# Banded attention in steps of two units instead of one, without the filling product, ahead of two fused MLPs

## The chip, the cores and the metric

One core of one Trainium2 chip runs the whole program. The metric is the device time of one execution in microseconds (us). The engines are TensorE (PE; its weight loads are PEld), VectorE (DVE), ScalarE (ACT), GpSimd (POOL) and SyncE (SP, which here only issues transfers). Each engine works through its own list of instructions in order and waits on semaphores for the others.

## What is computed

Attention over 2 batches and 8 heads of 768 tokens by 64, in which a token sees the 96 latest tokens and the first 8, with a slope per head; then two MLPs over all 1536 tokens. Cut to what matters:

```
scores = q @ k.T / sqrt(D) + bias        # bias: -slope[h] * distance
scores = where(is_global | is_local, scores, -1e9)
a = exp(scores - max);  a = a / (sum(a) + 1e-9)
x = a @ v                                 # (1536 tokens, 512)
h = x @ w_in;  x = (h * tanh(softplus(h))) @ w_out
x = rms_norm(x) * rms_g
out = (silu(x @ w_gate) * (x @ w_val)) @ w_out2
```

## The kernel before

**Units.** Attention goes by units: a unit is one batch b, one pair of heads p (two heads j = 0, 1) and one tile t of 128 queries. A pair has six units, and there are 2 x 4 pairs, so 48 units. Because of the band, a unit with t = 0 has 128 keys and any other 256 (`width`). A unit passes through seven pieces of work: `scores` (TensorE, L639, one product per head into two score banks), `soft` (VectorE L660 adds the bias and takes the row's maximum; ScalarE L670 does the exponential and its sum; each once per head), `norm` (VectorE L685 and L687 make the inverse of the sums, GpSimd L689 multiplies, once per head), `transp` (TensorE L704, four transposes, two for t = 0), `evac` (ScalarE L712 copies the transposed unit out of its bank), `pv` (TensorE L724, the products with the values, into a bank that three units share) and, after the third unit of such a bank, `evac_out`: `split_into` writes the bank as a rounded high part (ScalarE L352) and a low part (VectorE L353, which reads L352's result). Behind each unit's scores TensorE also issues a filling product of 128 x 128 at L647 into the unused end of a score bank; its result is not used.

**The loop.** The loop at L757 runs i from -4 to 49. In loop i the engines get the scores of unit i + 4, the transposes of unit i, the value products of unit i - 2, the evacuation of unit i - 1, the softmax of unit i + 3, the norm of unit i + 2 and the `evac_out` of unit i - 2, written in that order. So the order of each engine's list is fixed by the loop's text. Score banks are two pairs that take turns.

**What is woven in.** Eight pieces of the first weights are converted during attention (`Piece`): mag, clamp, b1, b2, b3, hi, lo, each one pass over 128 x 512 words. `plan` gives each a loop and a slot, and `tick` issues it there. Here mag is on ScalarE (L152), clamp, b1, b2, b3 on VectorE (L160, L163, L169, L175), hi and lo on GpSimd. mag and b3 also issue the transfer of a later weight piece on SP. The transfers of q, k and v of later pairs stand in SP's list too.

**The end.** In its last loops, by `AHEAD`, TensorE also does the first 16 groups of three products of the first MLP (L362). `mish1(0)` is ScalarE's and VectorE's part of the MLP's first half step. What follows, from the first product at L414 on, is the two MLPs.

Of the kernel before, what the change touches and what calls it, by code (L numbers as in the profile page):

```python
# [17 lines left out]
P = 128  # L18
B, H, S, D = 2, 8, 768, 64
NT = S // P  # L20
# [23 lines left out]
AHEAD = {-4: (0, 2), -3: (2, 4), -2: (4, 6), -1: (6, 8), 0: (8, 12), 1: (12, 16)}  # L44
# [6 lines left out]
def tile_attention_mish_swiglu(  # L51
# [74 lines left out]
    class Piece:  # L126
# [16 lines left out]
        def mag(self):  # L143
# [443 lines left out]
    def attention_banded():  # L587
        fresh()
        mm = [mm_bank() for _ in range(4)]
        with ExitStack() as st:  # L590
            qk = st.enter_context(tc.tile_pool(name="a_qk", bufs=2, reuse_waits="tile"))
            bp = st.enter_context(tc.tile_pool(name="a_b", bufs=1, reuse_waits="tile"))
            sm = st.enter_context(tc.tile_pool(name="a_s", bufs=5, reuse_waits="tile"))
            ep = st.enter_context(tc.tile_pool(name="a_e", bufs=5, reuse_waits="tile"))
            pp = st.enter_context(tc.tile_pool(name="a_p", bufs=3, reuse_waits="tile"))
# [31 lines left out]
            sc, ex, pt, po = {}, {}, {}, {}  # L627
# [5 lines left out]
            def scores(u):  # L633
                b, p, t = u
                n = width(t) // P
                banks = mm[2:4] if units.index(u) % 2 else mm[0:2]
                for j in range(2):
                    r = slice(64 * j, 64 * j + 64)
                    pe.matmul(  # L639
                        banks[j][:, 0 : n * P],  # L640
                        qs[b, p][r, t * P : (t + 1) * P],
                        ks[b, p][r, 0, :] if t == 0 else ks[b, p][r, t : t + NT : NT - 1, :],
                        start=True,
                        stop=True,
                    )

                pe.matmul(  # L647
                    banks[1][:, 3 * P :], ones[:, 0:P], ones[:, 0:P], start=True, stop=True
                )
                sc[u] = banks  # L650

            def soft(u, tick):
                b, p, t = u
                n = width(t)
                banks = sc.pop(u)
                e = ep.tile([P, 2, 2 * P], F32, tag="e", name=nm("e"))
                s = sm.tile([P, 4, 2], F32, tag="s", name=nm("s"))
                for j in range(2):
# [18 lines left out]
                    )  # L677
                    tick(j)
                ex[u] = (e, s)

            def norm(u, tick):
                b, p, t = u
                n = width(t)
# [271 lines left out]
```

## Time and profile before

| | |
|---|---|
| Runs shown | 690.1, 689.78, 693.67 us; median 690.1 |
| Profiled execution, its own time | 688.42 us, span 686.6 us |
| TensorE's products, busy | 669.5 us, 98% of the span |
| TensorE's weight loads, busy | 587.1 us, 86% |
| VectorE busy | 450.2 us, 66% |
| ScalarE busy | 385.9 us, 56% |
| GpSimd busy | 68.2 us, 10% |
| TensorE's mean granted clock | 0.997 of full speed |

The shares are means over stages that differ: attention is roughly the first sixth of the span. A busy TensorE is not TensorE at its peak, since products overlap and their ends are modelled; the starts of its weight loads tell its pace better. In the chain of waits each piece is what the next one had to wait for.

### The profile page before, as it was taken

Reading aid. Unit: us, or ns where it says so; the run is one execution under the profiler, and the core shown is the slowest. Engines: PE = TensorE matmul, PEld = TensorE weight load, DVE = VectorE, ACT = ScalarE, POOL = GpSimd, SP = SyncE. Lnnn points to the kernel's source line nnn. Section 1 sums busy time; section 2 is a strip of 40 time slices with the busy share of each in tenths; the row PEclk is TensorE's granted clock in tenths of the full one; section 3 lists DMA queues with packets and bytes.
Section 4 is the critical chain, followed back from the end, with each engine's and each line's share of the span. In section 5 each row is a group of like instructions: output and inputs, shape, how many; then the busy total and the mean of one; then the engine's idle time right before and its main releaser. Section 6 shows DMA issues by size and latency. Waiting matters only on the chain.

```text
span 686.6 us, 10023 instructions
## 1 busy us (share of the span) xinstructions
PE 669.5 (98%) x3760; PEld 587.1 (86%) x3760; DVE 450.2 (66%) x1067; ACT 385.9 (56%) x722; POOL 68.2 (10%) x128
## 2 busy tenths in 40 slices
PE   7999999999999999999989999999999999999997
PEld 3656678999999999999868899999999999999996
DVE  6777865887788778877777778873368774331232
ACT  5888879888888888888888423222122222111111
POOL 3666750000000000000000000000000000000000
PEclk9999999999999999999999999999999999999999
DMA  7967520122113113211212122130022200010111
GB/s 237 304 224 223 160 84 32 67 89 86 67 62 93 62 61 93 63 62 62 84 40 63 42 81 93 62 93 31 1 62 92 93 1 1 0 47 1 46 47 51
DMA packets 26728, 54.20 MB, mean 79 GB/s; under 512 B 2608, under 2 KB 14640, under 8 KB 26672
## 3 DMA queue, kind: packets, MB, share of 16 engines
q1 hardware_dynamic: 25968, 53.16, 24.4%
q8 instruction: 31, 0.51, 0.3%
q10 hardware_dynamic: 704, 0.33, 0.2%
q14 instruction: 25, 0.20, 0.1%
HBM read 50.34 MB, written 3.15 MB: 78 GB/s over the span
## 4 chain that ended last, share of the span: by engine, by line
PE 84%; ACT 7%; DVE 6%; DMA 1%; issue 1%; SPq 0%; DVEq 0%
PE mm L362 45%; PE s L414 31%; PE mm L639 2%; PE s L724 2%; ACT e L670 2%; PE s L704 2%; DVE x L426 1%; ACT s L460 1%; DVE e L660 1%; DMA q<-in_qT_dram 1%; PE mm L273 1%; PE s L443 1%; DVE hl L353 1%; ACT hl L352 1%; PE mm L647 1%
## 5 line engine op out<-in xcount | busy, mean ns | idle before, releaser
L362 PE MATMUL mm<-hl,w 128*128 128x384 f32 x1920 | 349.2, 336 | 0.0
L362 PEld LDWEIGHTS mm<-hl,w 128*128 128x128 f32 x1920 | 336.8, 188 | 7.5 <-issue 1.0
L414 PE MATMUL s<-w,g 128*128 128x512 f32 x1008 | 247.5, 395 | 0.0
L414 PEld LDWEIGHTS s<-w,g 128*128 128x128 f32 x1008 | 188.5, 189 | 36.3
L552 ACT ACTIVATE r<-mm 128x384 f32<-128x384 f32 x48 | 23.5, 490 | 128.5 <-PE mm L362 128.5
L553 DVE TENSOR_TENSOR r<-r,mm 128x384 f32<-128x384 f32 x48 | 26.4, 549 | 65.9 <-ACT r L552 65.9
L426 DVE TENSOR_TENSOR x<-x,s 128x512 f32<-128x512 f32 x60 | 40.4, 687 | 41.0 <-PE s L414 41.0
L488 ACT ACTIVATE g<-r 128x384 fp32r<-128x384 f32 x48 | 25.2, 526 | 68.4 <-DVE r L553 68.4
L391 DVE TENSOR_TENSOR d<-d,mm 128x384 f32<-128x384 f32 x64 | 32.5, 549 | 42.0 <-ACT d L388 42.0
L689 POOL TENSOR_SCALAR e<-e,s 128x256 f32<-128x256 f32 (+1 forms) x96 | 47.6, 508 | 35.3 <-DVE bias L620 10.0
L670 ACT ACTIVATE e<-e,s 128x256 f32<-128x256 f32 (+1 forms) x96 | 46.1, 482 | 7.9 <-DVE s L660 7.6
L169 DVE SCALAR_TENSOR_TENSOR bits<-stage,bits 128x512 int32<-128x512 int32 x68 | 48.2, 709 | 2.1
L175 DVE SCALAR_TENSOR_TENSOR bits<-stage,bits 128x512 int32<-128x512 int32 x68 | 47.2, 694 | 2.0
L488 ACT ACTIVATE g<-d 128x384 fp32r<-128x384 f32 x64 | 33.6, 526 | 21.6 <-DVE d L391 20.0
L492 DVE TENSOR_TENSOR g<-r,g 128x384 fp32r<-128x384 f32 x48 | 26.8, 559 | 28.4 <-ACT g L488 28.4
L386 ACT ACT_TABLE_LOAD x32 | 41.1, 1283 | 0.6
L194 DVE TENSOR_TENSOR w<-bits,w 128x512 fp32r<-128x512 f32 x60 | 41.3, 689 | 0.0
L382 ACT ACTIVATE d<-mm 128x384 f32<-128x384 f32 x64 | 30.5, 491 | 18.7 <-PE mm L362 17.1
L382 ACT ACT_TABLE_LOAD x31 | 39.8, 1283 | 0.5
L190 ACT ACTIVATE w<-bits 128x512 fp32r<-128x512 f32 x60 | 37.0, 616 | 0.0
L639 PE MATMUL mm<-k,q 64*128 64x256 f32 (+1 forms) x168 | 31.9, 411 | 4.7 <-DVE s L660 2.6
L660 DVE CUSTOM_DVE_ANT_0 e<-mm,bias 128x256 f32<-128x256 f32 (+1 forms) x96 | 35.0, 395 | 0.8 <-PE mm L639 0.8
(82 smaller groups left out, 506.2 us busy)
## 6 DMA issues: line engine op xcount, KB each, us to landing
stage<-in_w_out_dram SPq DMA_DIRECT2D x28, 512.0 KB, 3.2
stage<-in_w_in_dram SPq DMA_DIRECT2D x16, 512.0 KB, 3.9
stage<-in_w_gate_dram SPq DMA_DIRECT2D x12, 512.0 KB, 3.4
stage<-in_w_val_dram SPq DMA_DIRECT2D x12, 512.0 KB, 3.5
k<-in_kT_dram SPq DMA_DIRECT2D x7, 704.0 KB, 4.2
out_dram<-x SPq DMA_DIRECT2D x12, 256.0 KB, 2.1
q<-in_qT_dram SPq DMA_DIRECT2D x7, 384.0 KB, 4.9
v<-in_v_dram SPq DMA_DIRECT2D x7, 384.0 KB, 6.1
```

The lines of the kernel that those rows point to most:

```text
L169: dve.scalar_tensor_tensor(self.bits, self.lw, 29, self.bits, op0=ALU.logical_shift_right, op1=ALU.bitwise_or,)
L175: dve.scalar_tensor_tensor(self.bits, self.hw, -1073741824, self.bits, op0=ALU.bitwise_and, op1=ALU.bitwise_or,)
L194: engine.tensor_tensor(self.wt[:, 1, :], self.fl, self.wt[:, 0, :].bitcast(F32), op=ALU.subtract)
L362: pe.matmul(ps[:, 0:BT], w[:, wi, col], xs[kc][:, xi, :], start=kc == 0 and i == 0, stop=kc == NK - 1 and i == 2,)
L382: act.activation(self.t[:, i, :], self.h[i], AF.Tanh, scale=0.5)
L414: pe.matmul(acc[m], gt[:, gi, tok], w[:, wi, :], start=c % 4 == 0 and i == 0, stop=c % 4 == 3 and i == 2,)
L426: dve.tensor_tensor(y, y, acc[m], op=ALU.add)
L488: act.activation(gt[:, 0, :], x, AF.Copy)
L639: pe.matmul(banks[j][:, 0 : n * P], qs[b, p][r, t * P : (t + 1) * P], ks[b, p][r, 0, :] if t == 0 else ks[b, p][r, t : t + NT : NT - 1, :] ...
L660: dve.tensor_tensor_reduce(e[:, j, 0:n], banks[j][:, 0:n], bias0[:, h, :] if t == 0 else bias[:, h, :], scale=-0.125, scalar=3.0e38, op0=A ...
L670: act.activation(e[:, j, 0:n], e[:, j, 0:n], AF.Exp, scale=-1.0, bias=s[:, 0, j : j + 1], accum_out=s[:, 1, j : j + 1],)
L689: pool.tensor_scalar(e[:, j, 0:n], e[:, j, 0:n], s[:, 3, j : j + 1], 0.0, op0=ALU.mult, op1=ALU.add,)
```

## The change

Attention goes by steps of two units (24 steps). A step's scores fill both halves of a head's score bank, k = 0 and 1. Loop i (from -2 to 24) has the scores of step i + 2, the transposes of step i (eight), the value products of step i - 1 (sixteen for full units: two units, two heads, two halves of the keys, each in two passes), then softmax of the first unit of step i + 2, evacuation of the first unit of step i, norm of step i + 1, softmax of the second unit, evacuation of the second, and `evac_out` of step i - 1. There is no filling product. All magnitudes are on VectorE. The slots of the pieces, the buffers, `AHEAD` and the place of `mish1(0)` follow the steps. The old L352, L353, L660, L670, L712, L362 and L414 become L349, L350, L659, L669, L706, L359 and L411.

```diff
-AHEAD = {-4: (0, 2), -3: (2, 4), -2: (4, 6), -1: (6, 8), 0: (8, 12), 1: (12, 16)}
+AHEAD = {-2: (0, 8), -1: (8, 12), 0: (12, 16)}
...
-            if self.i < NW_EARLY:
-                act.activation(self.fl, self.hw.bitcast(F32), AF.Abs)
-            else:
-                dve.tensor_scalar(
-                    self.bits, self.hw, 1, 1,
-                    op0=ALU.logical_shift_left, op1=ALU.logical_shift_right,
-                )
+            dve.tensor_scalar(
+                self.bits, self.hw, 1, 1,
+                op0=ALU.logical_shift_left, op1=ALU.logical_shift_right,
+            )
...
-                pe.matmul(
-                    banks[1][:, 3 * P :], ones[:, 0:P], ones[:, 0:P], start=True, stop=True
-                )
...
+                banks = mm[2:4] if i % 2 else mm[0:2]
+                for k, (b, p, t) in enumerate(steps[i]):
+                    n = width(t)
+                    for j in range(2):
+                        r = slice(64 * j, 64 * j + 64)
+                        pe.matmul(
+                            banks[j][:, 2 * k * P : 2 * k * P + n],
+                            qs[b, p][r, t * P : (t + 1) * P],
...
+                i0 = 1 + k * (ns - 4) // NW_EARLY
+                for op, di, slot in (
                     ("mag", 0, 0),
-                    ("clamp", 1, 2),
-                    ("b1", 2, 0),
-                    ("b2", 2, 2),
-                    ("b3", 3, 1),
-                    ("hi", 3, 3),
-                    ("lo", 4, 3),
+                    ("clamp", 0, 1),
+                    ("b1", 0, 2),
+                    ("b2", 1, 0),
+                    ("b3", 1, 1),
+                    ("hi", 1, 2),
+                    ("lo", 2, 1),
                 ):
...
-            for i in range(-4, nu + 2):
+            for i in range(-2, ns + 1):
...
+                ahead = i + 2 < ns
+                if ahead:
+                    scores(i + 2)
                 if i < 0:
                     warm(bank("s3"), WARM, ones)
...
+                if 0 <= i < ns:
+                    transp(i)
+                if i >= 1:
+                    pv(i - 1)
...
+                if i == ns - 1:
                     mish_first = Mish(first)
...
+                    for c in range(2):
+                        mish_first.tanh(c)
+                if ahead:
+                    soft(i + 2, 0)
+                tick(0)
+                if 0 <= i < ns:
+                    evac(i, 0)
+                if 0 <= i + 1 < ns:
+                    norm(i + 1)
+                tick(1)
+                if ahead:
+                    soft(i + 2, 1)
+                if 0 <= i < ns:
+                    evac(i, 1)
+                if -1 <= i < 5:
+                    make_bias(i + 3)
+                if i >= 1:
+                    evac_out(i - 1)
+                tick(2)
...
-                if i == nu - 1:
+                if i == ns - 1:
                     for piece in pieces:
                         piece.rest()
-                if i == nu:
                     mish1(0, mish_first)
```

ScalarE in the middle of attention, before, around the split of the second value bank of pair (0, 3) (`hl_181`; `e` are the units' exponentials, `pt` their evacuated transposes, "x2" is once per head):

```order
L712 ACTIVATE pt_936<-s_170_902 128x512
L670 ACTIVATE e_938,s_939<-e_938,s_939 128x256 x2
L712 ACTIVATE pt_961<-s_176_929 128x2x128
L670 ACTIVATE e_963,s_964<-e_963,s_964 128x256 x2
L352 ACTIVATE hl_181<-s_171_907 128x384
L712 ACTIVATE pt_988<-s_180_952 128x512
```

The same place in the change, from the split of that pair's first value bank on:

```order
L349 ACTIVATE hl_177<-s_128_765 128x384
L669 ACTIVATE e_842,s_843<-e_842,s_843 128x256 x2
L706 ACTIVATE pt_865<-s_139_844 128x2x128
L669 ACTIVATE e_842,s_843<-e_842,s_843 128x256 x2
L706 ACTIVATE pt_865<-s_140_847 128x512
L349 ACTIVATE hl_181<-s_134_810 128x384
```

Between two splits of neighbouring steps stand two units' exponentials and two evacuations; the split is the last of its step.

VectorE at that place, before (`ISA` is the reduction of L660, its second row the read of its accumulator):

```order
L660 ISA e_963,s_964<-mm_190,bias 128x256
L660 ISA s_964 128x1
L163 TENSOR_SCALAR bits_918<-bits_918 128x512
L660 ISA e_963,s_964<-mm_191,bias 128x256
L660 ISA s_964 128x1
L685 TENSOR_SCALAR s_939<-s_939 128x2
L169 SCALAR_TENSOR_TENSOR bits_918<-stage_559,bits_918 128x512
L687 RECIPROCAL s_939<-s_939 128x2
L353 TENSOR_TENSOR hl_181<-s_171_907,hl_181 128x384
L660 ISA e_990,s_991<-mm_192,bias 128x256
```

VectorE there in the change, behind the two reductions of the step's first unit:

```order
L166 SCALAR_TENSOR_TENSOR bits_819<-stage_492,bits_819 128x512
L680 TENSOR_SCALAR s_795<-s_795 128x4
L681 RECIPROCAL s_795<-s_795 128x4
L172 SCALAR_TENSOR_TENSOR bits_819<-stage_492,bits_819 128x512
L659 ISA e_842,s_843<-mm_190,bias 128x256
L659 ISA s_843 128x1
L659 ISA e_842,s_843<-mm_191,bias 128x256
L659 ISA s_843 128x1
L350 TENSOR_TENSOR hl_181<-s_134_810,hl_181 128x384
L659 ISA e_897,s_898<-mm_192,bias 128x128
```

L350 stands behind the reductions of both units, and the next step's reductions stand behind L350.

TensorE, before, one unit of pair (0, 1):

```order
L639 MATMUL mm_192<-k_210,q_209 128x256
L639 MATMUL mm_193<-k_210,q_209 128x256
L647 LDWEIGHTS x_85
L647 MATMUL mm_193<-x_85 128x128
L704 MATMUL s_75_400<-ident,e_322 128x128 x4
L724 MATMUL s_76_405<-pt_381,x_84 64x128 x4
```

and one step of pair (0, 2)'s scores in the change:

```order
L640 MATMUL mm_192<-k_294,q_293 128x256
L640 MATMUL mm_193<-k_294,q_293 128x256
L640 MATMUL mm_192<-k_294,q_293 128x256
L640 MATMUL mm_193<-k_294,q_293 128x256
L697 MATMUL s_88_507<-ident,e_403 128x128 x4
L697 MATMUL s_89_512<-ident,e_403 128x128 x4
L720 MATMUL s_83_471<-pt_483,v_297 64x128 x4
L720 MATMUL s_90_521<-pt_483,v_297 64x128 x4
```

Two units of one kind of work now stand together, and L647 is gone.

## Rows read from the trace of the kernel before

**Rows 1.** The head of the page.
```profile
span 686.6 us, 10023 instructions
```

**Rows 2.** Windows: stretch, length, busy by engine, granted clock, transfers' share, GB/s.
```profile
15.37:83.22 67.85, 65.47 (x577) 41.40 (x577) 52.46 (x249) 59.52 (x194) 46.06 (x83) 1.00 0.78 234
...
110.24:686.60 576.36, 566.55 (x2929) 521.35 (x2928) 372.96 (x694) 297.18 (x445) 5.19 (x8) 1.00 0.18 57
```

**Rows 3.** Timeline of TensorE (start, length, instructions): a pair's first scores.
```profile
83.22 0.49 PE L639 MATMUL mm<-k,q 64*128 64x128 f32 x4
```

**Rows 4.** Timeline of TensorE's weight loads for one unit, with idle time before.
```profile
64.26 0.30 PEld L639 LDWEIGHTS mm<-k,q 64*128 64x128 f32 x4 [0.17 <-DVE s L687]
64.89 0.10 PEld L647 LDWEIGHTS <-x 128*128 128x128 bf16 x1 [0.33 <-issue]
64.91 0.42 PEld L704 LDWEIGHTS s<-ident,e 128*128 128x128 f32 x4
65.50 0.42 PEld L724 LDWEIGHTS s<-pt,v 128*64 128x64 f32 x8 [0.17 <-issue]
66.08 0.30 PEld L639 LDWEIGHTS mm<-k,q 64*128 64x128 f32 x4 [0.17 <-issue]
```

**Rows 5.** The chain that ended last, in order of time: start, length, piece.
```profile
59.49 0.27 ACT pt L712
59.75 0.98 ACT e L670 x4
...
61.14 0.56 DVE hl L353
...
76.30 0.48 ACT pt L712
...
105.24 2.29 PE mm L362 x12
...
114.52 4.18 PE mm L362 x24
```

**Rows 6.** Waits, 0 to 135 us: total, times, longest.
```profile
DVE hl L353 <- ACT hl L352: 16.1, 15, 2.8
```

**Rows 7.** Timeline of ScalarE and VectorE around L352 and L353, and the first magnitude.
```profile
16.57 0.67 ACT L152 ACTIVATE bits<-stage 128x512 f32<-128x512 f32 x1 [1.56 <-DMA stage<-in_w_in_dram]
...
60.14 0.50 ACT L670 ACTIVATE e<-e,s 128x256 f32<-128x256 f32 x1
...
60.63 0.48 ACT L352 ACTIVATE hl<-s 128x384 fp32r<-128x384 f32 x1
...
61.14 0.56 DVE L353 TENSOR_TENSOR hl<-s,hl 128x384 fp32r<-128x384 f32 x1 [0.52 <-ACT hl L352]
61.62 0.42 DVE L660 CUSTOM_DVE_ANT_0 e<-mm,bias 128x256 f32<-128x256 f32 x1
...
62.08 0.51 ACT L670 ACTIVATE e<-e,s 128x256 f32<-128x256 f32 x1 [0.48 <-DVE s L660]
```

**Rows 8.** Lines by form, 0 to 135 us: count | busy us, mean ns | idle before.
```profile
L685 DVE TENSOR_SCALAR s<-s 128x2 f32<-128x2 f32 x48 | 11.1, 230 | 3.3 <-ACT e L670 3.2
...
L169 DVE SCALAR_TENSOR_TENSOR bits<-stage,bits 128x512 int32<-128x512 int32 x12 | 9.3, 778 | 0.1
...
L175 DVE SCALAR_TENSOR_TENSOR bits<-stage,bits 128x512 int32<-128x512 int32 x11 | 7.8, 707 | 0.1
...
L670 ACT ACTIVATE e<-e,s 128x128 f32<-128x128 f32 x16 | 6.2, 391 | 0.0
...
L160 DVE TENSOR_SCALAR bits<-bits 128x512 f32<-128x512 f32 x12 | 5.1, 421 | 0.1
```

**Rows 9.** Windows: stretch, length, busy by engine, granted clock, transfers' share, GB/s.
```profile
13.00:15.00 2.00, 0.29 (x3) 0.05 (x1) 1.93 (x12) 2.00 (x7) 1.45 (x4) 1.00 0.99 383
...
344.00:348.00 4.00, 0.71 (x5) 0.40 (x4) 3.90 (x9) 3.90 (x10) 0.20 (x1) 1.00 0.00 0
348.00:352.00 4.00, 4.00 (x13) 3.17 (x12) 1.89 (x3) 3.96 (x6) 1.21 (x1) 0.58 0.36 117
```

More of the change, by code (lines that the diff above doesn't have):

```diff
@@ L626, in attention_banded @@
             ]
-            sc, ex, pt, po = {}, {}, {}, {}
+            steps = [units[i : i + 2] for i in range(0, len(units), 2)]
+            ns, per = len(steps), NT // 2
+            ex, pt, po = {}, {}, {}
             first = []
@@ L678, in soft @@
[L678 to L683, printed above, removed]
-                e, s = ex[u]
-                dve.tensor_scalar(s[:, 2, :], s[:, 1, :], 1.0e-9, None, op0=ALU.add)
-                tick(2)
-                dve.reciprocal(s[:, 3, :], s[:, 2, :])
-                for j in range(2):
-                    pool.tensor_scalar(
-                        e[:, j, 0:n], e[:, j, 0:n], s[:, 3, j : j + 1], 0.0,
-                        op0=ALU.mult, op1=ALU.add,
-                    )
@@ L732, in evac_out, with norm @@
-            def evac_out(u):
-                b, p, t = u
-                hf, m = divmod(t, TB)
-                if m == TB - 1:
-                    split_into(xs[2 * b + hf][p], po.pop(u)[:, 0:BT])
-            nu = len(units)
+                        bias=s[:, 0, k, j : j + 1],
+                        accum_out=s[:, 1, k, j : j + 1],
+                    )
+            def norm(i):
+                e, s, _ = ex[i]
+                dve.tensor_scalar(s[:, 2], s[:, 1], 1.0e-9, None, op0=ALU.add)
+                dve.reciprocal(s[:, 3], s[:, 2])
+                for k, (b, p, t) in enumerate(steps[i]):
+                    n = width(t)
+                    for j in range(2):
+                        pool.tensor_scalar(
+                            e[:, k, j, 0:n], e[:, k, j, 0:n], s[:, 3, k, j : j + 1], 0.0,
+                            op0=ALU.mult, op1=ALU.add,
+                        )
@@ new lines, in transp @@
+            def transp(i):
+                e = ex.pop(i)[0]
+                pt[i] = []
+                for k, (b, p, t) in enumerate(steps[i]):
+                    tr = bank(f"s{k}").rearrange("p (j c q) -> p j c q", j=2, c=2)
+                    for j in range(2):
+                        for c in range(width(t) // P):
+                            pe.transpose(
+                                tr[:, j, c, :], e[:, k, j, c * P : (c + 1) * P], ident
+                            )
+                    pt[i].append(tr)
@@ L739, in attention_banded, with evac_out @@
+            def evac_out(i):
+                for b, p, t in steps[i]:
+                    hf, m = divmod(t, TB)
+                    if m == TB - 1:
+                        split_into(xs[2 * b + hf][p], po[hf][:, 0:BT])
             for b, m in ((bias0, base0), (bias, base)):
@@ L761, in tick @@
                         pieces[k](op)
-                if i + 4 < nu:
-                    scores(units[i + 4])
+                ahead = i + 2 < ns
+                if ahead:
+                    scores(i + 2)
                 if i < 0:
                     warm(bank("s3"), WARM, ones)
-                if 0 <= i < nu:
-                    transp(units[i])
-                if i >= 2:
-                    pv(units[i - 2])
-                for j in range(*AHEAD.get(i - nu, (0, 0))):
+                if 0 <= i < ns:
+                    transp(i)
+                if i >= 1:
+                    pv(i - 1)
+                for j in range(*AHEAD.get(i - ns, (0, 0))):
                     c, kc = divmod(j, NK)
```

130 lines of the change are left out of this document (48 added, 82 removed).

## The prediction

> **What bounds the kernel now.** The profiled execution's span is 686.6 us [rows 1] and its own time 688.42 us; the change touches only what TensorE does before its first product at L414. I read the windows first: from 110.24 us to the end TensorE is busy 566.6 of 576.4 us [rows 2], and none of that is edited, so I take it as a constant. Everything hangs on when 110.24 is reached. From 15.37 (the transfer of the second pair's q and k has just landed) to 83.22 (the first scores of a pair again, six pairs on [rows 3]) are 67.85 us for 36 units: 11.31 us a pair of heads, 5.65 us per three units.
>
> Two things compete there. TensorE's own pace is read from its weight loads: scores at 64.26, filling product at 64.89, transposes at 64.91, value products at 65.50, next scores at 66.08 [rows 4]: 1.82 us a unit, hence at most 10.9 us a pair, less for the shorter t = 0 unit. So TensorE alone does not explain 11.31, though it is busy 65.5 of 67.85 us.
>
> The chain of waits shows the other: around 60 us it runs through ScalarE's exponentials, the split of the value bank, VectorE's L353, and only then back to TensorE [rows 5]. The waits say the same: VectorE stands 16.1 us, in 15 pieces, at L353 because ScalarE's L352 is late [rows 6]. The timeline gives one turn: exponential at 60.14, the next ScalarE instruction (L352) at 60.63, L353 at 61.14, the next reduction at 61.62, its exponential at 62.08 [rows 7]. As VectorE runs its list in order, the next unit's reductions stand behind L353, and ScalarE, which needs them, idles.
>
> **A timetable for before, to see whether that is the whole story.** From one L353 to the next, three units: L353 to reduction 0.48, to exponential 0.46, then three pairs of exponentials at 0.98 [rows 5], two evacuations at 0.48 [rows 5] (the third lies beside L353), then 0.51 from L352 to L353. Sum 0.48 + 0.46 + 2.94 + 0.96 + 0.51 = 5.35. ScalarE also does eight magnitudes (0.67 [rows 7], less 0.10 of overlap, so 0.57) in 42 units, 0.33 per three units: 5.68. Measured: 5.65. So this loop through L352 and L353, not TensorE, sets the pace, and I cost the change by it.
>
> **What the change does to that loop.** A step has two units. By the order rows ScalarE does two exponentials, evacuation, two exponentials, evacuation, and only then L349 (the old L352); VectorE does all four reductions, the two small norm operations and up to three piece operations, and then stands at L350 (the old L353). Before, the wait came after one unit's work; now it comes after two. It comes as often: twice in three steps. What stands behind L350 is the next step's four reductions, and with them ScalarE.
>
> Piece operations, each 0.08 less than its mean because the next starts that early (61.14 + 0.56 against 61.62 [rows 7]): clamp and b1 0.34 each, b2 0.70, b3 0.63 [rows 8]. The magnitude moves from ScalarE to VectorE; I cost it at clamp's row, as both are the same kind of operation. A loop is of kind A (magnitude, clamp, b1; loops 1, 3, 6, 8, 11, 13, 16, 18), B (b2, b3; the loop after each) or plain. Norm I take as 0.30: 0.23 mean for its first half [rows 8], 0.15 for the reciprocal, less overlap. Two reductions: 0.70 (half for t = 0).
>
> A loop with i mod 3 = 0, counted from where VectorE starts it: first exponential 0.46, two of them 0.98, evacuation of a t = 0 unit 0.27 [rows 5], two more 0.98, evacuation 0.48, 0.51, L350 0.48: 4.16. But the second unit's first exponential needs its reduction, ready at 0.70 + 0.30 + 0.46 = 1.46 in a plain loop, 2.14 in A, 2.79 in B, against 1.71 when ScalarE is free: waits of 0, 0.43, 1.08. A's b1 stands behind L350: 0.34 more. So 4.16, 4.93, 5.24.
>
> The other two loops of a pair have one such wait, at the end of the second: 0.46 + 0.78 (two t = 0 exponentials at 0.39 [rows 8]) + 0.48 + 0.98 + 0.48, then 2 x 0.98 + 2 x 0.48 + 0.51 + 0.48: 7.09. The second unit's wait is 0, 0.15 or 0.80 by kind; 0.45 more where B follows A; b1 0.34 where the second loop is A. With the kinds in order the seven pairs from loop 1 to 21 come to 12.62, 12.82, 13.47, 12.67, 11.85, 12.62 and 12.05: 88.1 us, 12.6 a pair against 11.31.
>
> **Ends.** The second pair's transfer gates the fourth step's scores as it gated unit 6, so at 15.37. VectorE starts on both units' scores, 0.85 later: 16.2. 16.2 + 88.1 = 104.3. The last evacuation of loop 21 ends about 0.8 before VectorE is there, so the transposes of loop 22 end at 103.9. Then come values 0.80 (one unit is t = 0), 24 products (4.18 [rows 5]), transposes 1.01, values 1.00, 12 products 2.29 [rows 5], values 1.00, 12 products 2.29: 12.6. The first L414 (L411 in the change) so stands at 116.5 instead of 110.24, **+6.3 us**. Mish's first half must be ready by then: its table load starts behind L349 of loop 23, about 5 us before, and is as long as now; I take it as just hidden, and cost nothing.
>
> **What TensorE gains, and why it does not count.** The 48 filling products cost 0.02 us each between weight loads [rows 4]. The idle stretches of its weight path at each change of kind are 0.33, 0.17 and 0.17 a unit [rows 4], and a step has one set instead of two. A step then needs between 3.6 (filling product only) and 2.95 us (one set saved too) against 3.65; I take 3.06: scores 0.63 + 0.43, transposes 0.59 + 0.42, values 0.58 + 0.42, where the second unit adds a unit's pace less its idle stretch [rows 4]. Either lies under 4.2, a third of 12.6, so it moves nothing before loop 22; in the tail the two ends differ by 0.6. The Trainium skill, page TensorEngine Tiling (Array Packing), section Tiling Modes, says that a change of tiling mode drains TensorE; the idle stretches agree, and by that rule alone the sum would be that of the first rival, 679 us.
>
> Step-wise, GpSimd gets four norm products at once instead of two; TensorE's transposes then wait for them, but they are needed only when ScalarE reaches its evacuation, over 1 us later. The magnitude also issues the next weight loads on SP, whose queue carries the same transfers in the same sequence; the first weights land at 16.57 [rows 7], and VectorE reaches its first magnitude at 16.9, so no wait comes in with it. Later transfers are asked for a pair or more ahead, and the pairs become longer.
>
> **The rivals.**
> 1. TensorE sets the pace, and the saved changes count. For it: TensorE shows as busy 65.5 of 67.85 us [rows 2], and each step saves up to 0.7. The pace is then what ScalarE and VectorE need without standing at L350: ScalarE 10 x 0.49 + 2 x 0.39 + 5 x 0.48 + 0.27 + 2 x 0.38 = 9.1 a pair, VectorE about as much, TensorE 8.6 to 10. At 9.5 to 10 a pair it is 1.3 to 1.8 less, over seven pairs some 11 us: 679. It decides where L350 waits under 0.9 us a time instead of the 1.7 to 2.3 of the timetable. Against it: 16.1 us at L353 already [rows 6], and the order rows.
> 2. The loop is as said, but pieces hide: VectorE reaches the second unit early because it enters most steps ahead of ScalarE. The waits by kind (b1 included) are 9.3 us of the 88.1 (seven pairs at 4.16 + 7.09 would be 78.8); without a third to two thirds of them the sum is +0 to +3: 690 to 693. For it: in the loops i mod 3 = 2 that is already so. Against it: after L350 both engines start even.
> 3. TensorE's clock falls to 1.2 GHz. In before it is at 1.00 (2.4 GHz) even from 13 to 15 us, where TensorE worked 0.29 of 2 us; it fell to 0.58 in 348 to 352 after 0.71 of 4 us [rows 9]. By the timetable each step has idle pieces up to 2 us. If it fell for most of the attention, a step of 3.05 would need up to 5.6 to 6.1, 1.4 to 1.9 over the 4.2, and 21 steps +30 to +40 us more: about 730.
> 4. The instructions are slower than in these rows, as VectorE and GpSimd overlap otherwise: 2 or 3% of 88 us, +2 or so. It lies in the main case's own range.
>
> **How the numbers follow.** The runs shown have a median of 690.1 us, 1.7 above the profiled execution's time; I add the 6.3 to that median: 696.4 us. Chances: the loop as worked out 0.60 (693 to 702), pieces hidden 0.24, TensorE's pace 0.09, the clock 0.07. The range 690 to 704 leaves out the fast rival and the clock. A measurement of this kernel can tell about 1%, that is 6.9 us; my forecast stands just under 697.0, and what the timetable leaves out (rival 4) adds more than it takes away, so I split the main case into 0.34 above and 0.26 below. Slower by over 1%: 0.34 + 0.07 = 0.41; within 1%: 0.26 + 0.24 = 0.50; faster by over 1%: 0.09.
>
> **What would show it.** Right: VectorE's waits at L350 for L349 sum to about 25 to 32 us in some 15 pieces, longest over 2; the chain around 60 us passes through ScalarE and VectorE with hardly any TensorE; pairs take 12 to 13.5 us; TensorE has idle pieces before transposes of 1 to 2 us; the first L414 stands near 116.5. Wrong: pairs of about 9.5 us with TensorE unbroken (rival 1), L350 waits as now or shorter (rivals 1 and 2), a granted clock below 1.00 before 100 us (rival 3), or a new gap between the last product at L362 and the first L414, if Mish comes late.

## The result and the profile after

| | before | after |
|---|---|---|
| Median of the runs timed together | 689.71 us (6 runs) | 699.81 us (6 runs) |
| Ratio, 95% interval | | 1.0129 [1.0103, 1.0155] |
| Profiled execution: own time, span | 688.42, 686.6 us | 699.79, 698.0 us |
| First product of the MLP behind the fused groups (L414, now L411) | 110.24 us | 120.82 us |
| From there to the end of the span | 576.36 us | 577.18 us |

The change makes the kernel 1.3% slower. Runs of one kernel differ with the mean clock that TensorE was granted: of the 58 runs of before beside the experiments, those at 0.997 or more, as the profiled one, took 688.4 to 689.75 us and those at 0.990 or less 692.2 to 693.4, and after's six had 0.983 to 0.991. Of the 11.4 us that the span grew, 10.6 lie ahead of the first L411 and 0.8 behind it, so attention is where the time went. The head of the page after, which answers to [rows 1], and its first row of busy times:

```profile
span 698.0 us, 9837 instructions
...
PE 661.3 (95%) x3710; PEld 586.6 (84%) x3710; DVE 446.9 (64%) x1027; ACT 381.4 (55%) x714; POOL 68.3 (10%) x128
```

TensorE's work shrank from 669.5 to 661.3 us, VectorE's and ScalarE's by 3.3 and 4.5 us, and GpSimd's stayed, so no engine got more to do. The windows of after (columns as in [rows 2]): five pairs of heads, from first scores to first scores, and the stretch behind the first L411.

```profile
15.44:80.70 65.26, 51.97 (x450) 35.80 (x451) 44.69 (x188) 45.26 (x150) 37.15 (x67) 0.93 0.73 216
120.82:698.00 577.18, 566.48 (x2929) 521.16 (x2928) 372.83 (x694) 297.00 (x445) 6.57 (x8) 1.00 0.18 57
```

65.26 us for five pairs are 13.05 a pair, against 11.31. TensorE works 52.0 of them, VectorE 44.7, ScalarE 45.3: no engine is near full, so they wait for each other. The waits of after from 0 to 135 us (total, times, longest), for [rows 6]:

```profile
DVE hl L350 <- ACT hl L349: 32.4, 15, 6.7
ACT e L669 <- DVE s L659: 25.1, 27, 2.3
```

The wait of the split doubled, 16.1 to 32.4 us. The longest of the fifteen, 6.7, stands in the tail (2.8 in before); the other fourteen have 25.7 us, 1.84 each, against 13.3 and 0.95 in before. ScalarE in turn now waits 25.1 us for VectorE's reductions, against 7.6. The chain of waits of after in one of these steps (start, length, piece), for [rows 5]:

```profile
49.60 0.48 ACT pt L706
50.08 1.06 ACT e L669 x4
51.13 0.48 ACT pt L706
51.62 0.39 ACT hl L349
...
52.03 0.56 DVE hl L350
52.58 0.42 DVE bits L160
...
53.09 0.42 DVE e L659
...
53.52 0.34 DVE e L659
...
53.87 0.60 DVE bits L166
```

And the same turn in VectorE's and ScalarE's timeline, for [rows 7] (the bracket is the idle time before):

```profile
52.03 0.56 DVE L350 TENSOR_TENSOR hl<-s,hl 128x384 fp32r<-128x384 f32 x1 [1.67 <-ACT hl L349]
...
53.56 0.51 ACT L669 ACTIVATE e<-e,s 128x256 f32<-128x256 f32 x1 [1.56 <-DVE s L659]
```

VectorE stands 1.67 us until ScalarE has done the step's second unit and L349. Then it splits, does a piece operation and the next step's reduction, and meanwhile ScalarE stands 1.56 us. The two take turns, and TensorE is not in this chain. The split after this one, of loop 9, begins at 57.70, 5.67 us later; that loop has two piece operations between its units. From the split of loop 20 to that of loop 21, which has none, it is 4.17 us. The row at 31.25 is the split of loop 3, the last of the first pair:

```profile
31.25 0.56 DVE L350 TENSOR_TENSOR hl<-s,hl 128x384 fp32r<-128x384 f32 x1 [1.44 <-ACT hl L349]
...
57.70 0.56 DVE L350 TENSOR_TENSOR hl<-s,hl 128x384 fp32r<-128x384 f32 x1 [1.67 <-ACT hl L349]
...
103.75 0.56 DVE L350 TENSOR_TENSOR hl<-s,hl 128x384 fp32r<-128x384 f32 x1 [2.68 <-ACT hl L349]
...
107.92 0.56 DVE L350 TENSOR_TENSOR hl<-s,hl 128x384 fp32r<-128x384 f32 x1 [1.97 <-ACT hl L349]
```

TensorE's weight loads in one step of after, for [rows 4]:

```profile
52.88 0.64 PEld L697 LDWEIGHTS s<-ident,e 128*128 128x128 f32 x6 [0.33 <-POOL w L191]
53.68 0.85 PEld L720 LDWEIGHTS s<-pt,v 128*64 128x64 f32 x16 [0.17 <-issue]
54.70 0.52 PEld L640 LDWEIGHTS mm<-k,q 64*128 64x128 f32 x8 [0.17 <-DVE s L680]
55.74 0.20 PEld L697 LDWEIGHTS s<-ident,e 128*128 128x128 f32 x2 [0.51 <-POOL e L685]
```

The idle stretches of 0.33, 0.17 and 0.17 us at a change of kind are the old ones, but they come once in a step of two units. What TensorE should save, it saves, and it then waits for others (0.51 in the last row, for GpSimd's norm product).

One thing is new. The granted clock of TensorE in after's windows (columns as above):

```profile
15.00:21.00 6.00, 5.56 (x32) 4.19 (x34) 2.66 (x14) 3.15 (x11) 2.28 (x5) 0.50 1.04 366
...
24.00:100.00 76.00, 58.27 (x520) 38.91 (x520) 53.83 (x230) 55.88 (x188) 47.55 (x86) 0.98 0.63 189
```

From 15 to 21 us TensorE runs at 0.50 of its clock (1.2 GHz) where before ran at 1.00. Later it falls for shorter stretches: 0.93 from 40 to 50 us and 0.90 from 50 to 60. The early fall is visible in the instructions as well; after's timeline of TensorE there:

```profile
15.44 1.65 PE L640 MATMUL mm<-k,q 64*128 64x128 f32 x8 [2.09 <-DMA q<-in_qT_dram]
17.02 1.97 PE L697 MATMUL s<-ident,e 128*128 128x128 f32 x8
18.92 1.55 PE L720 MATMUL s<-pt,x 128*64 128x128 f32 x12
```

The tail of after in TensorE's timeline, with no gap between the last fused products and L411, so Mish's first half was hidden:

```profile
118.61 2.37 PE L359 MATMUL mm<-hl,w 128*128 128x384 f32 x12
120.82 3.38 PE L411 MATMUL s<-w,g 128*128 128x512 f32 x14
```

### The profile page after: what moved, and what is told of

The parts are those of the page before. It is cut to its first block, busy times and chain, and to the rows that moved or that the text cites. A ratio compares the mean times of both kernels' runs of the same rounds, so it can differ in the third digit from the quotient of the medians.

```text
span 698.0 us, 9837 instructions
## 1 busy us (share of the span) xinstructions
PE 661.3 (95%) x3710; PEld 586.6 (84%) x3710; DVE 446.9 (64%) x1027; ACT 381.4 (55%) x714; POOL 68.3 (10%) x128
## 4 chain that ended last, share of the span: by engine, by line
PE 78%; DVE 10%; ACT 9%; issue 2%; DMA 1%; SPq 0%; DVEq 0%; ACTq 0%
PE mm L359 44%; PE s L411 30%; ACT e L669 3%; DVE e L659 2%; DVE x L423 1%; ACT pt L706 1%; ACT s L457 1%; DVE bits L166 1%; DMA q<-in_qT_dram 1%; DVE bits L172 1%; PE s L720 1%; PE s L440 1%; ACT hl L349 1%; PE mm L640 1%; DVE bits L160 1%
## 5 line engine op out<-in xcount | busy, mean ns | idle before, releaser
L359 PE MATMUL mm<-hl,w 128*128 128x384 f32 x1920 | 348.3, 336 | 0.0
L359 PEld LDWEIGHTS mm<-hl,w 128*128 128x128 f32 x1920 | 336.9, 188 | 7.0 <-issue 0.5
L411 PE MATMUL s<-w,g 128*128 128x512 f32 x1008 | 247.4, 395 | 0.0
L411 PEld LDWEIGHTS s<-w,g 128*128 128x128 f32 x1008 | 188.3, 189 | 36.4
L669 ACT ACTIVATE e<-e,s 128x256 f32<-128x256 f32 (+1 forms) x96 | 46.1, 481 | 25.5 <-DVE s L659 25.1
L697 PE MATMUL s<-ident,e 128*128 128x128 f32 x176 | 32.2, 297 | 21.1 <-ACT pt L706 13.1
L697 PEld LDWEIGHTS s<-ident,e 128*128 128x128 f32 x176 | 19.4, 146 | 36.8 <-POOL e L685 33.6
L685 POOL TENSOR_SCALAR e<-e,s 128x256 f32<-128x256 f32 (+1 forms) x96 | 45.3, 489 | 48.5 <-ACT e L669 24.2
L166 DVE SCALAR_TENSOR_TENSOR bits<-stage,bits 128x512 int32<-128x512 int32 x68 | 47.1, 693 | 2.1
L172 DVE SCALAR_TENSOR_TENSOR bits<-stage,bits 128x512 int32<-128x512 int32 x68 | 46.8, 688 | 2.0
L485 ACT ACTIVATE g<-d 128x384 fp32r<-128x384 f32 x64 | 33.6, 526 | 22.0 <-DVE d L388 20.1
L191 DVE TENSOR_TENSOR w<-bits,w 128x512 fp32r<-128x512 f32 x60 | 41.3, 689 | 0.0
L659 DVE CUSTOM_DVE_ANT_0 e<-mm,bias 128x256 f32<-128x256 f32 (+1 forms) x96 | 34.1, 394 | 6.1 <-PE mm L640 5.9
```

The costliest lines, as they stand in the source:

```text
L166: dve.scalar_tensor_tensor(self.bits, self.lw, 29, self.bits, op0=ALU.logical_shift_right, op1=ALU.bitwise_or,)
L172: dve.scalar_tensor_tensor(self.bits, self.hw, -1073741824, self.bits, op0=ALU.bitwise_and, op1=ALU.bitwise_or,)
L191: engine.tensor_tensor(self.wt[:, 1, :], self.fl, self.wt[:, 0, :].bitcast(F32), op=ALU.subtract)
L359: pe.matmul(ps[:, 0:BT], w[:, wi, col], xs[kc][:, xi, :], start=kc == 0 and i == 0, stop=kc == NK - 1 and i == 2,)
L411: pe.matmul(acc[m], gt[:, gi, tok], w[:, wi, :], start=c % 4 == 0 and i == 0, stop=c % 4 == 3 and i == 2,)
L485: act.activation(gt[:, 0, :], x, AF.Copy)
```

## The experiments

The theory: the loop through L349 and L350 sets the pace of attention, because the split stands behind both units' work on both engines, and the pieces between lengthen it; the early fall of the clock adds about 3 us in the first pair. Rivals: TensorE's clock is lost all along because the fillers are gone; the pieces hide; the magnitudes on VectorE are what costs; TensorE's own work is the bound. Each ratio is to the kernel before, timed beside it on the same chip; products that warm or fill have results that nobody uses.

**1. Fill again.** Two filling products ahead of each step's scores.

```diff
                 banks = mm[2:4] if i % 2 else mm[0:2]
+                for _ in range(2):
+                    pe.matmul(
+                        banks[1][:, 3 * P :], ones[:, 0:P], ones[:, 0:P], start=True, stop=True
+                    )
```

> The change with its filling products put back: two products of 128 x 128 per step, now ahead of the step's scores in the bank that these overwrite. Theory 1 (the loop through L349 and L350 sets the pace, and the rest of the loss is a granted clock that fell to 0.50 from about 14.7 to 21.3 us because TensorE had idle pieces from 5 us on): a filling product lasts 0.06 us and fills no idle piece, so the clock falls as in the change and the time is 699 to 701 us. Theory 2 (the missing filling product is what lets the clock fall): clock 1.00 throughout attention, first L411 3 to 4 us earlier than 120.8, 696 us.

Measured: 698.78 us, ratio 1.0109 [1.0086, 1.0132], first L411 at 121.17, waits at L350 32.3 us. The granted clock still fell, to 0.62 from 14 to 18 us, 0.83 from 30 to 40 and 0.68 from 70 to 80. So the missing filler is not why the change is slower, and two fillers a step don't hold the clock, though the first fall was shorter here (loop 3's split at 29.58 instead of 31.25 us).

**2. Warm the start.** Products beside the first transposes, so that TensorE does not stand while the second pair's q is on its way.

```diff
                 if i < 0:
-                    warm(bank("s3"), WARM, ones)
+                    warm(bank("s3"), 3, ones)
+                if i == 0:
+                    warm(bank("s3"), 4, ones)
                 if 0 <= i < ns:
                     transp(i)
+                if i == 0:
+                    warm(bank("s3"), 8, ones)
```

> The change with more warming products (128 x 512, results not used) in the first loops alone: three instead of one in loops -2 and -1, four ahead of and eight behind the transposes of loop 0, where TensorE stands for GpSimd and for the second pair's q. Theory 1 says that the clock falls at 14.7 because of the idle pieces from 5 to 15 us: here it stays at 1.00 to 21 us, the first pair of the loop (15.4 to 28.0 us in the change) takes about 9.6 to 10.5 instead of 12.6 us, as the timetable has it at full clock, and the time is about 697 us. If the clock is not what the first pair lost, it stays 12.6 us long and 699.8 us.

Measured: 697.02 us, 1.0094 [1.0073, 1.0116]. TensorE's timeline and windows of this kernel:

```profile
15.86 0.93 PE L640 MATMUL mm<-k,q 64*128 64x128 f32 x8 [0.82 <-DMA q<-in_qT_dram]
16.71 1.09 PE L697 MATMUL s<-ident,e 128*128 128x128 f32 x8
17.73 0.88 PE L720 MATMUL s<-pt,x 128*64 128x128 f32 x12
```

```profile
14.00:24.00 10.00, 8.52 (x75) 5.60 (x73) 5.74 (x27) 7.22 (x26) 5.56 (x12) 1.00 1.07 337
...
32.00:40.00 8.00, 7.03 (x56) 5.14 (x56) 4.57 (x25) 6.12 (x21) 4.98 (x11) 0.79 0.26 59
```

The clock stays at 1.00 through the first pair, its products take 0.93, 1.09 and 0.88 us instead of 1.65, 1.97 and 1.55, and the second pair of the loop starts its scores at 25.75 instead of 28.02: 2.3 us. Later the clock falls elsewhere, and only 0.7 of it is left at the first L411 (120.15, in a profiled run of 698.38 us): loops 4 to 6 take 13.41 us from split to split against 12.63 in after, with the clock at 0.79 from 32 to 40 us. That this clock is what they lost by is argued. The one of the six runs with a mean clock of 0.998 took 695.88 us, 7.5 above the profiled run of before (688.42, at 0.997), where the forecast has 6.3. The waits at L350 stay at 32.3 us. So the clock accounts for most of the lateness of the first pair, and not for the waits at the split.

**3. Split later, in after and in before.** The split of a full bank is moved into the next loop, where both halves stand near its head: ScalarE's half ahead of its exponentials, VectorE's behind the first unit's reductions. In after:

```diff
+                late = 2 <= i < ns - 1
+                if late:
+                    evac_half(i - 2, False)
                 if ahead:
                     soft(i + 2, 0)
+                if late:
+                    evac_half(i - 2, True)
                 tick(0)
...
-                if i >= 1:
+                if i >= ns - 1:
                     evac_out(i - 1)
```

In before the same: the high part ahead of `evac`, the low part behind `soft`, one loop later.

> The change with the split of the value bank one loop later and at the head of the loop: ScalarE's high part ahead of the step's exponentials, VectorE's low part behind the first unit's two reductions; the last two banks as before. Nothing else differs. Theory 1 (the wait at L350 sets the pace): the waits of the low part for the high part nearly vanish (32.4 us in the change), the timetable gives 11.3 us a pair instead of 12.6, the first L411 comes some 9 us earlier, near 111 us, and the time is 690 to 692 us. Rival (TensorE's waits for GpSimd's norm products, 33.6 us at the transposes, set the pace): the pairs stay at 12.6 us and the time at 699 us.

> The kernel before with the same single edit: the split of the value bank one loop later, its high part at the head of ScalarE's loop, its low part behind the unit's two reductions. If before is paced by the loop through L352 and L353, the pairs go from 11.3 to 10.3 us, where TensorE's own 1.82 us a unit takes over, the first L414 stands near 103 instead of 110.2, and the time is 682 to 684 us. If TensorE paced before already, it stays at 689 to 690 us.

Measured: after with it 690.44 us, 0.9992 [0.9976, 1.0009], first L411 at 113.39; before with it 683.59 us, 0.9901 [0.9878, 0.9924], first L414 at 106.57. The waits at the split fall from 25.7 to 8.3 us in after (without the tail's 6.7) and from 13.3 to 4.1 in before (without the tail's 2.8 and now 3.7). The row of before with the later split, 0 to 135 us:

```profile
DVE hl L745 <- ACT hl L749: 4.1, 9, 0.9
```

The place of the split costs the change about 9 us and costs even the kernel before 6.5. That is the loop of the theory, undone. Before's pairs now take 10.31 us (scores at 31.97, 42.28 and, two pairs later, 62.90), and its chain from 40 to 80 us is TensorE alone. In the profiled run of this kernel the early clock falls too (0.63 from 14 to 18 us), filling products and all, and its first L414 comes 3.5 us behind the 103 that I expected (in the sixth experiment, with the clock at 1.00, it comes at 103.45). After's pairs take 11.8 us on the mean of five instead of the 11.3 expected. With the later split in both kernels, the change is still 6.9 us the slower one (690.44 against 683.59): the wait at the split bounds either kernel, but behind it the two-unit steps meet other limits, which the next experiments look for.

**4. Pieces out of the way.** In after the piece operations of a step go behind the second unit and L350, with the split where the change put it, and then with the later split.

```diff
                     soft(i + 2, 0)
-                tick(0)
                 if 0 <= i < ns:
                     evac(i, 0)
...
-                tick(1)
...
                     evac_out(i - 1)
+                tick(0)
+                tick(1)
                 tick(2)
```

> The change with only the weight pieces moved: all of a loop's piece operations on VectorE behind the second unit's reductions and the split's low part, instead of between the two units. Theory 1 (the loop through L349 and L350): what the pieces no longer take ahead of the second unit's exponentials they now take behind L350, ahead of the next step's reductions, where ScalarE idles too. The timetable gives 118.9 instead of 116.7 for the first L411, so some 2 us more than the change: 701 to 702 us. Rival (the prediction's second: the pieces between the units are what ScalarE waits for): up to 9 us less, 691 to 695 us.

> Both edits: the split of the value bank one loop later at the head of the loop, and the piece operations behind the second unit's reductions. Nothing then stands between VectorE and ScalarE's next exponentials. The timetable gives 9.6 to 10.1 us a pair and the first L411 (120.8 in the change) near 98 at full clock, 101 with the clock's early fall: 678 to 682 us. If GpSimd's norm products (TensorE's waits at the transposes) limit the steps as soon as the loop through L350 is gone, the pairs stay above 11 us and the time near 690 us.

Measured: alone 703.78 us, some 2 more than expected, 1.0195 [1.0168, 1.0222], first L411 at 126.59, waits at L350 35.1 us. With the later split 685.43 us, 0.9925 [0.9899, 0.9951], first L411 at 107.76. The same edit costs 4 us in one kernel and gains 5 in the other. A piece behind L350 stands whole between the split and the next reductions; ahead of the second unit at least a part may lie beside ScalarE's work, so this alone does not show that the pieces weren't hidden where the change put them. After's own trace does: loops 15 and 21, without pieces on VectorE, take 4.18 and 4.17 us from split to split, loop 9, with two pieces between the units, 5.67, as the timetable has it (4.16 and 5.58, the latter being its 5.24 and the 0.34 of the b1 behind the split of loop 8). The combination fell short of the 678 to 682 us that I expected. Part of that may be the clock: its nine runs go from 682.62 us, at a mean clock of 0.999, to 688.65, at 0.990. TensorE still waits 22.1 us at L697 for GpSimd's norm products, the limit that the expectation named as its rival, and its pairs take 11.0 us on the mean of five, just at that rival's bound.

**5. All three.** Later split, later pieces and the warm start; and then the value products of step i - 1 put ahead of the transposes of step i, which gives GpSimd one more us in each step.

```diff
+                if i >= 1:
+                    pv(i - 1)
                 if 0 <= i < ns:
                     transp(i)
...
-                if i >= 1:
-                    pv(i - 1)
```

> The same with the early warming products of the earlier run (results not used), which kept the granted clock at 1.00 to 22 us: about 3 us less than without, 676 to 679 us. If the clock then falls later in attention instead, the gain is smaller.

> The kernel with later split, later pieces and warming products, with TensorE's value products of step i - 1 put ahead of the transposes of step i instead of behind them. Theory A (GpSimd's four norm products in a row, 0.61 us each, set the pace there): the transposes are asked for about 1.0 us later in a step, so TensorE's waits at L697 for L685, 20.4 + 6.7 us there, fall by at least 8 us, the first L411 stands 1 to 3 us before 106.2, and the time is 681 to 683.3 us. Theory B (VectorE's and ScalarE's own work sets the pace, GpSimd is only late beside it): the waits at L697 fall too, but the value products wait for ScalarE's evacuation instead, and the time stays within 1 us of 684.3 or is longer.

Measured: 684.29 us, 0.9913 [0.989, 0.9935], first L411 at 106.22, the clock at 1.00; with the values first 683.84 us, 0.9913 [0.9891, 0.9935], first L411 at 105.26. The first missed what I expected by more than 5 us. Its norm products by form (count | busy us, mean ns | idle before) and a piece of its chain:

```profile
L685 POOL TENSOR_SCALAR e<-e,s 128x256 f32<-128x256 f32 x80 | 47.6, 611 | 12.8 <-PE s L720 4.5 <-DVE s L681 3.2 <-ACT e L669 3.0
```

```profile
57.99 2.31 POOL e L685 x3
```

Four of these products in a row take 2.4 us; in after they took 502 ns each. The chain from 40 to 85 us has them with 26.7%. I read GpSimd as the new bound, and the second kernel shows that this was too simple. Its waits, 0 to 135 us:

```profile
PEld s L720 <- ACT pt L706: 15.7, 22, 1.4
...
PE s L720 <- ACT pt L706: 10.0, 18, 1.1
```

TensorE hardly waits at L697 for L685 any more (1.0 us in its weight loads, where it was 20.4), and it waits at the values for ScalarE's evacuation instead, 15.7 us in its weight loads. (The 10.0 us of its products are mostly the same idle time seen twice, so the two are not added; that holds too for the 20.4 and 6.7 us which my expectation names together.) The chain there from 40 to 80 us has L659 with 19.4% and L669 with 17.4%, and TensorE hardly. The time, 683.84 us, is in the range of theory B and 0.5 above that of A, which is less than the interval can tell, and the first L411, 1.0 us earlier, is at the edge of A; but what the values wait for now is what B named. I read it so that GpSimd's products and the loop through VectorE and ScalarE are near-equal limits; no run took both away.

**6. The best of before.** The kernel before with the later split and ten warming products behind loop 1's transposes, and the same without the filling product.

```diff
                 if 0 <= i < nu:
                     transp(units[i])
+                if i == 1:
+                    warm(bank("s3"), 10, ones)
```

> The kernel before with the split one loop later (683.6 us) and ten warming products of 128 x 512 (results not used) behind the transposes of loop 1, where TensorE stands 2.5 us for the second pair's q and the granted clock then fell to 0.5 until 22 us. Clock theory: it stays at 1.00, the first L414 comes near 103.5 instead of 106.6, 680 to 681 us. If the fall has another cause, 683 to 684 us.

> The kernel before with the later split and the warming products behind loop 1's transposes (681.6 us, paced by TensorE alone), now without the 48 filling products. Here TensorE's time counts in full: by the starts of the weight loads a filling product costs 0.02 us, by its share of the chain of waits 0.16 us. So 680.5 us by the first, 674 us by the second. If the filling products held the clock, 684 us or more.

Measured: 681.56 us, 0.9872 [0.9847, 0.9897], first L414 at 103.45; without the filling product 681.76 us, 0.9866 [0.9844, 0.9887], first L414 at 103.03. The clock is 1.00 in both. The chain of the first from 40 to 80 us by line, and one unit of its weight loads:

```profile
by line: PE mm L639 34.3%; PE s L724 31.6%; PE s L704 24.5%; PE mm L647 9.7%
```

```profile
51.44 0.30 PEld L639 LDWEIGHTS mm<-k,q 64*128 64x128 f32 x4 [0.17 <-DVE s L660]
52.07 0.10 PEld L647 LDWEIGHTS <-x 128*128 128x128 bf16 x1 [0.33 <-issue]
52.08 0.42 PEld L704 LDWEIGHTS s<-ident,e 128*128 128x128 f32 x4
52.67 0.42 PEld L724 LDWEIGHTS s<-pt,v 128*64 128x64 f32 x8 [0.17 <-issue]
```

The second without the filling product:

```profile
51.05 0.30 PEld L639 LDWEIGHTS mm<-k,q 64*128 64x128 f32 x4 [0.17 <-DVE s L657]
51.68 0.42 PEld L701 LDWEIGHTS s<-ident,e 128*128 128x128 f32 x4 [0.33 <-issue]
52.27 0.42 PEld L721 LDWEIGHTS s<-pt,v 128*64 128x64 f32 x8 [0.17 <-issue]
52.86 0.30 PEld L639 LDWEIGHTS mm<-k,q 64*128 64x128 f32 x4 [0.17 <-DVE s L684]
```

Now TensorE alone is the chain, at 1.82 us a unit. Both kernels beat before and after by over 1%. The chain gives the filling product 9.7% of the stretch, 0.16 us a unit, and I had costed its removal at 680.5 us by the loads or 674 by the chain; but without it a unit takes 1.81 us instead of 1.82: the idle 0.33 us at that place is there with it and without it. A share of the chain is what stood there, not what would go if it went.

**7. The filling product and the magnitudes, each alone.** Before without the filling product, and after with the magnitudes on ScalarE, as before had them.

```diff
-                pe.matmul(
-                    banks[1][:, 3 * P :], ones[:, 0:P], ones[:, 0:P], start=True, stop=True
-                )
```

```diff
-            dve.tensor_scalar(
-                self.bits, self.hw, 1, 1,
-                op0=ALU.logical_shift_left, op1=ALU.logical_shift_right,
-            )
+            if self.i < NW_EARLY:
+                act.activation(self.fl, self.hw.bitcast(F32), AF.Abs)
+            else:
+                dve.tensor_scalar(
...
```

> The kernel before without its 48 filling products and nothing else. Theory 1 (the loop through L352 and L353 paces before, and a filling product takes TensorE 0.02 to 0.06 us): the time stays within 1 us of before, 689 to 691 us, and the pairs at 11.3 us. Rival (the filling products hold the granted clock): it falls more often in attention, 693 us or more.

> The change with its eight magnitudes back on ScalarE, where they stand between the first unit's exponentials and its evacuation. The timetable gives 118.0 instead of 116.7 for the first L411: about 1 us more than the change, 700 to 702 us. If moving them to VectorE was what made the change slow, 695 us or less.

Measured: 689.12 us, 0.9989 [0.997, 1.0009], with 17.2 us of waits at L353; and 703.86 us, 1.0186 [1.016, 1.0211], first L414 at 125.97. The filling product of before costs nothing that the interval shows, and gives nothing. The magnitudes were right to move: on ScalarE the change would be 4 us slower still. I expected 700 to 702 us; the granted clock from 24 to 100 us was 0.93 there against 0.98, which goes the same way, but no run separates the two.

## Why the prediction was right, and which term was too small

I forecast 696.4 us and 690 to 704; it is 699.81.

- **The bound was named rightly.** Splitting later takes 9 us out of the change and 6.5 out of the kernel before; nothing else that I tried without it moved either kernel by more than about 4. It is not the only limit of the two-unit steps: without it the change is still 6.9 us slower than before without it.
- **The timetable held where it was a timetable.** Its last split, in loop 21, should begin 0.48 ahead of 104.3, at 103.8. It began at 107.92. The split of loop 3, the first pair's last, should begin at 16.2 + 12.62 less the 0.34 of b1 and the 0.48 of the split, 28.0. It began at 31.25. So the six pairs between took 76.7 us against 75.8, and the tail from there to L411 12.9 against 12.7. Counted from split to split, four of the six pairs came within 0.2 us. The other two ran over, 13.03 against 12.67 and 12.83 against 11.85, and in each of these L680, which stands ahead of the second unit's reductions, took 1.2 us instead of the usual 0.17, beside an L191 on GpSimd (rows in the last section). That is rival 4, VectorE and GpSimd overlapping otherwise, in two single places; that the pairs lost their time by it is argued from VectorE's list.
- **The mis-sized term is the first pair: +3.2 us.** I took its products at the lengths of [rows 4], at full clock, and took from [rows 9] that a stand of about 2 us there leaves the clock alone. The stand was as long as before (2.09 us against 2.10), but the clock fell to 0.50. VectorE began 1.76 us behind the first scores instead of 0.85, and then stood 2.19 us for the next step's scores, where the timetable has no wait (0.23 in the second experiment, at full clock). Why the clock fell stays open. What TensorE did ahead of it differs: from 10 to 13 us it was busy 1.97 of 3 us in after and 3.00 in before (windows of after, then of before). The change has two loops ahead of loop 0 with a warming product in each, where before had four.

```profile
10.00:13.00 3.00, 1.97 (x13) 0.93 (x10) 2.48 (x15) 3.00 (x14) 1.71 (x4) 1.00 0.88 251
```

```profile
10.00:13.00 3.00, 3.00 (x21) 1.57 (x22) 2.93 (x18) 2.92 (x12) 2.08 (x5) 1.00 0.87 242
```

  But that can't be all of it: the kernel before without the filling product was busy 3.00 of those 3 us too and stood 2.13, and its clock fell to 0.75 from 14 to 18 us. So rival 3 came true, in a stretch of 6 us instead of most of attention. The warm start gives back 2.3 us of the 3.2; of the other 0.9, 0.5 is that its first scores stand at 15.86 instead of 15.37, and the rest stays open.
- **The sum:** 6.3 as forecast, 3.2 for the first pair, 0.9 for six pairs and 0.2 for the tail are the 10.6 us that the first L411 came later than the old L414 in the two profiled runs. The medians lie 10.1 apart and not 11.4, because other runs of before have less clock than the profiled one; so the forecast, which starts from before's median, missed by 3.4.
- **The check on before flatters the timetable.** It takes all three units at full width. With the t = 0 unit at the lengths used for the change (exponentials 0.39, evacuation 0.27), the mean of three units is 0.2 less, 5.5 against the 5.65 measured, 3% short instead of within 1%.
- **The chances leaned the wrong way.** I gave 0.50 to within 1%, with 0.24 of it for pieces that hide. They don't: the loops of after with pieces are as much longer as the timetable says.
- **What would show it:** waits at L350 of 25 to 32 us (32.4), the chain without TensorE and pairs of 12 to 13.5 came, but for one pair (12.63, 13.82, 13.03, 12.83, 12.11 and 12.25 from split to split). TensorE's stands ahead of the transposes were shorter than the 1 to 2 us named: 33.6 us in 46 of them, 1.6 the longest. The gap ahead of L411 did not. The clock below 1.00 ahead of 100 us, named as a sign of error, did, and was most of the error.
- **TensorE's savings** are real and idle. The page TensorEngine Tiling (Array Packing) of the Trainium skill, section Tiling Modes, says that a change of mode drains TensorE; the weight loads agree (0.33, 0.17 and 0.17 us at each change of kind, half as many changes in after). By that rule alone the change would have gained; it only can where TensorE sets the pace, and in two-unit steps no kernel here got there: with later split, later pieces and warm start TensorE's weight loads still waited 20.4 us at L697 for GpSimd. In one-unit steps it got there, with the later split alone.

## What to carry to other kernels

When two in-order engines hand a small piece of work to each other once per step, its place in their lists can set the pace of the whole loop: look for what stands behind the waiting instruction, and move the hand-over to where both halves are long ready (a loop later, at the head) before making steps larger. Here a larger step saved only on TensorE, which did not set the pace, and doubled a wait that comes twice in three steps. A timetable by rows of the trace held to about 1% over six pairs, so look first at what it assumes at full clock: a change's start-up, and how much the clock of the profiled run differs from that of the other runs.

## What the runs showed of the hardware that I had not expected

**A clock that falls or not at equal stands.** Seven of the profiled runs stand 2.0 to 2.5 us for the same transfer near 13 us. Before (2.10 us) keeps 1.00; the six others fall to 1.2 GHz, among them after (2.09), before without the filling product (2.13) and before with the later split (2.50). The last two were busy 3.00 of the 3 us from 10 to 13, as before was. The windows of before without the filling product:

```profile
14.00:18.00 4.00, 2.59 (x16) 1.71 (x16) 1.97 (x13) 2.46 (x8) 1.80 (x4) 0.75 1.02 381
```

So neither the length of the stand nor the work of those 3 us separates the kernels that fall from the one that doesn't, and as the runs of one kernel differ in their mean clock (0.989 to 0.998 for before), it may be the run as much as the kernel; no trace shows the early clock of a second run of the same kernel. All five kernels that put products into the stand kept 1.00 through the first 24 us. In before with the later split these products were worth about 2 us, 683.59 against 681.56, and its runs lie closer together (680.98 to 682.5 us, where they went from 682.13 to 685.98).

**A tiny instruction of 1.2 us.** L680 on four columns takes 165 ns at the median. In after's timelines of VectorE and of GpSimd:

```profile
61.20 1.23 DVE L680 TENSOR_SCALAR s<-s 128x4 f32<-128x4 f32 x1
...
74.99 1.24 DVE L680 TENSOR_SCALAR s<-s 128x4 f32<-128x4 f32 x1
```

```profile
60.97 1.44 POOL L191 TENSOR_TENSOR w<-bits,w 128x512 fp32r<-128x512 f32 x1
```

The first L680 began after GpSimd's L191 and ended with it (62.43 and 62.41), and so did the second, beside an L191 that began at 74.50 and took 1.71 us (76.23 and 76.21). The Trainium skill, page SBUF — State Buffer, section Who interferes with whom, says that VectorE in a 2-port mode contends with GpSimd for a pair of ports that they share, that whoever issues first has it for the whole instruction, that the other is blocked, and that `tensor_scalar` is among the operations that can enter such a mode. These rows agree; in which mode L680 ran, they don't show. The norm products on GpSimd, 502 ns in after and 611 in the fifth experiment, where VectorE is busier (60.67 against 53.83 of 76 us), may come from the same, but no run took VectorE's work away to show it.
